# Denominators apart from numerators, feature weights reordered by GpSimd, and a reshuffled plan in a gated mix of two attentions

## The chip, the core and the metric

The kernel runs on one core of one Trainium2 chip. The metric is the device time of one execution in microseconds (us). The core has five engines that run at the same time: TensorE (PE) multiplies matrices, its weight loads being shown apart as PEld; ScalarE (ACT) does exponentials; VectorE (DVE) and GpSimd (POOL) do elementwise work; SyncE (SP) issues most of the transfers (DMAs). Results of PE go to eight PSUM banks, everything else lies in SBUF.

## The reference

The inputs are 2048 tokens of 512 features, in 32 heads of 16.

```python
g = sigmoid((x * gate_w).sum(-1, keepdims=True))
# A: softmax attention
q, k, v = heads(x @ A_wqkv)
a = softmax(q @ k.T * Dh**-0.5) @ v          # per head, 2048 x 2048 scores
a = merge(a) @ A_wo
# B: linear attention with a learnt feature map
q, k, v = heads(x @ B_wqkv)
pq, pk = q @ w_phi, k @ w_phi                # per head, 16 x 16
phi_q = concat(softmax(pq), softmax(-pq)); phi_k = the same of pk
kv, z = phi_k.T @ v, phi_k.sum(tokens)       # per head, 32 x 16 and 32
b = merge(phi_q @ kv / (phi_q @ z + 1e-6)) @ B_wo
out = g * a + (1 - g) * b
```

## The kernel before

**Branch A.** A score unit is 128 keys by 512 queries of one head; four heads side by side make a pack (one 32-row strip of PE each), 16 packs make a group, and there are 32 groups, 512 packs, 2048 units. PE computes the scores of two units (`_qk`, matmul at line 993) into a ring of four PSUM banks, ACT takes the exponential of both at once into `ET` (`_exp`, line 1041), and PE multiplies the result with the values into the accumulator of the group (`_pv`, `_values`, line 1100). Some units take another way: PE computes their scores into one of the other four banks (`vqk`), DVE forms the exponential's bits (line 900) and corrects them (`v_step`, line 925), and PE multiplies the result (`vs`) with the values (`pvx`). How many of a group's 64 units go to DVE is the list `NUMS` (line 847). A finished group is transposed out of PSUM by DVE (line 1121), normalised, brought back by SP's transfers and multiplied with `WoA`.

**Branch B.** The weights of q and k are first multiplied with the feature weights `wphi` (`_b_fuse`, line 1216): eight groups of four matmuls, whose moving operand is `wphi`, 128 columns each. Head and feature order is changed by the way in which the matmul reads `wphi`. Then, for pairs of 128-token tiles, `_b_pair` computes the features: a projection, POOL's negation (line 1274), maxima and subtraction on DVE, an exponential on ACT (line 1283), sums on DVE and POOL, POOL's reciprocals and ratios (`_b_ratio`), and a product on DVE (line 1329). Eight pairs are keys (`_b_kv` accumulates them); eight pairs are queries, which SP transposes into `phiT` (`_b_phit`, line 1388). `_b_kvbd` masks the accumulated sums into `kvbd`: for each of eight groups of four heads, 68 columns, in which each head has 16 numerator columns and one denominator column behind them. `_b_num` makes, for each tile of queries and each half of the heads, four matmuls of 68 columns into one bank (line 1406); DVE then forms the denominators (line 1418), takes reciprocals (1426) and multiplies (1427) into `onB`, which SP transposes (line 1450) for the matmul with `WoB`.

**The order of the work** is not written by hand. Each operation is given an engine, a cost, dependencies, and a rank `prio`, mostly a due time counted in packs (`K0`, `Q0`, `NDUE`, `QDUE`, `KDUE`, `VDUE`). `Plan.order` simulates the five queues with these costs, takes at each step what can start first, and among what can start then the lowest rank; the outcome is five fixed queues, in which each instruction waits for semaphores. PE's fill (matmuls with a zero operand, line 1107, and pads, line 1013) is added where the streaming of the last `SPAN` us would fall under the shares `SHARE`, `FLOOR` or `PAD`. `_late` keeps other PE work from delaying the next scores. `c_pe(n)`, line 531, is the planner's cost of a matmul of n columns.

Of the kernel before, what the change touches and what calls it, by code (L numbers as in the profile page):

```python
# [7 lines left out]
ALU = mybir.AluOpType  # L8
AX = mybir.AxisListType

P = 128
# [54 lines left out]
class Plan:  # L66
# [6 lines left out]
    SWITCH, PASS, STEP = 0.105, 0.2155, 0.004  # L73
    SPAN, SHARE, FILL = 3.3, 0.55, 0.2155
    PAD, PADS, OVER = 0.45, 3, 0.1
    SLIP, GAPS, FLOOR = 0, 0.7, 0.44

# [32 lines left out]
    def op(self, eng, fn, cost, reads=(), writes=(), deps=(), name="", prio=0.0, rel=-99, kind="full",  # L110
# [27 lines left out]
        return o  # L138

    def _late(self, end):  # L140

        k = self.n_qk
        if k >= len(self.qks) > 0:
            x = self.exps[-1]
            if self.last.end is not None or x.end is None and self.exps[-2].end is None:
                return False
            done = self.exps[-2].end + x.cost if x.end is None else x.end
            return end > done + self.LAT["ACT"] + self.MORE["ACT", "PE"] - self.SWITCH + self.TAIL
        if k < 2 or any(d.end is None for d in self.qks[k].deps):
            return False  # L150
        x = self.exps[k - 1]
        if x.end is None:
            if self.exps[k - 2].end is None or any(d.end is None for d in x.deps):
                return False
            done = max([self.exps[k - 2].end] + [d.end + d.lat for d in x.deps]) + x.cost
        else:
            done = x.end
        return end > done - self.LAT["PE"] - self.PASS - self.SWITCH + self.SLIP

    TAIL = 9.0  # L160
    NEAR = 0.05
    SAME = 100
    OPEN = 2
    HURRY, FREE = 20, 20
    PORT = ("v_step", "b_neg", "b_max", "b_sub", "b_sum", "b_total", "b_mul", "n_mul", "n_den", "kvbd")
# [230 lines left out]
class _Kernel:  # L396
# [9 lines left out]
    URGENT, AHEAD, SOON, REST = 4, -(1 << 30), 4, 6  # L406
    QDUE, KDUE, VDUE = 24, 17, 11
    P_Q, P_MUL, P_NEG = 1, 1, 1
    P_REC, P_SUM = 0, 4
    P_BACK, RATIO, BV = 1, 1, 8  # L410
    P_M, P_BMUL, CHUNKS = 0, 0, 2
    GDUE = 26
# [4 lines left out]
    LAST, FIRST_OUT, NEXT_OUT, DEP_OUT = 0, 8, 0, 2  # L417
    ALONE, EARLY = 12, 6
    PVP = 10
# [13 lines left out]
    def build(self):  # L433
        with ExitStack() as ctx:
            self._memory(ctx)
            p = self.plan
            p.pad = lambda ot: lambda e: self._fill(e, ot)
            p.free_banks = [(b, 0.0, []) for b in range(self.NRING, 8)]
            self._loads()
            self._consts()  # L440
            self._projections()
            self._branch_b()
            self._attention()
            p.qks, p.exps = self.qks, self.exps
            p.order()
            p.finals = self.stores
            p.emit(self.nc, ctx)
# [132 lines left out]
    def _consts(self):  # L580
# [29 lines left out]
        self.b_wphi0 = B()  # L610
        z = op("POOL", lambda e: e.memset(self.wphi[:], 0.0), 0.6, prio=-30)
        parts = []
        phi = self.B_w_phi.rearrange("(c h) d f -> h d c f", h=8)
        for hh in range(8):
            parts.append(lambda e, hh=hh: e.dma_start(self.wphi[16 * hh:16 * hh + 16, :, 16 * hh:16 * hh + 16], phi[hh]))
        self._shared_dma("wphi", parts, self.b_wphi, -5, [z])
        self.dma("SP", "wob", lambda e: e.dma_start(self.WoB[:], self.B_wo.rearrange("(q p) n -> p q n", p=P)),
# [228 lines left out]

    NUMS = (6, 10, 12, 14, 14, 16, 13, 15, 14, 17, 16, 13, 17, 15, 19, 16, 11, 18, 14, 17, 19, 14, 17, 14, 15, 20, 14, 20, 12, 16, 20, 14)

    def _plan_vector(self):

        NT, away = self.NT, []
        for g in range(self.NPACK // NT):
            n = self.NUMS[g]
            away += [4 * (NT * g + 1 + (2 * k + 1) * (NT - self.REST) // (2 * n)) + (len(away) + k) % 4 for k in range(n)]
        batches = [away[k:k + self.PACK] for k in range(0, len(away), self.PACK)]
        self.hooks = {}
        for k, units in enumerate(batches):
            due = max(units[0] / 4 - self.LEAD, self.VMIN)
            self.hooks.setdefault(max(0, int(due) - 4), []).append(
                lambda k=k, units=units, due=due: self._vector_batch(k, units, due))  # L860
        for n in range(1, 4 * self.NQC):
            self.hooks.setdefault(max(0, 32 * n - 30), []).insert(0, lambda n=n: self._proj_q(*divmod(n, 4)))
        self.away = set(away)
# [291 lines left out]

    NDUE = 23
    K0, SK, Q0, SQ = 30.0, 11.5, 214.0, 15.25

    def _branch_b(self):
# [6 lines left out]
        self.b_kv = [B() for _ in range(2)]  # L1166
        self.b_kvbd, self.b_onB, self.b_rinvB = B(), [B(), B()], [B(), B()]
        self.b_numB, self.b_numR = [B(), B()], B()
# [24 lines left out]
        for ch in range(NQC):  # L1193
            for tt in (0, 2):
                t = 4 * ch + tt
                due = self.Q0 + self.SQ * t
                phi = self._b_pair(0, t, due)
                for k in range(2):
                    self._b_phit(tt + k, phi, k, due + 12 + 2 * k)
                    self._b_num(t + k, self._num_due(t + k))  # L1200
                    self._b_out(tt + k)
# [4 lines left out]
    def _b_fuse(self, s, due):  # L1206
# [4 lines left out]
        for c in range(4):  # L1211
            job = Job()

            def mm(e, c=c, job=job):
                for cp in range(4):
                    ins = e.matmul(self._bank(job)[:, P * cp:P * cp + P], self.WT[:, cp, P * c:P * c + P],  # L1216
                                   self.wphi[:, cp, :].rearrange("p (g i f) -> p g f i", g=2, i=4), start=True, stop=True)
                return ins
# [24 lines left out]
    def _b_pair(self, s, t0, due):  # L1243
# [25 lines left out]
        def chain(ops, off, bufs):  # L1269
            for name, cost, fn, *spare in ops:  # L1270
# [5 lines left out]
                self.P_NEG * 1.1),  # L1276
               ("b_max", two(1024), lambda e: e.tensor_tensor(tree, x[:, :, 0:8], x[:, :, 8:16], ALU.max))]  # L1277
              + [("b_max", two(128 * n), lambda e, n=n: e.tensor_tensor(tree[:, :, 0:n], tree[:, :, 0:n],
                                                                       tree[:, :, n:2 * n], ALU.max)) for n in (4, 2, 1)]
              + [("b_sub", two(2048), lambda e: e.tensor_tensor(x, x, spread(tree[:, :, 0]), ALU.subtract))],  # L1280
# [3 lines left out]
           name="b_exp", prio=due + 1)  # L1284
        chain([("b_sum", two(1024), lambda e: e.tensor_tensor(half, x[:, :, 0:8], x[:, :, 8:16], ALU.add))]  # L1285
              + [("b_sum", two(128 * n), lambda e, n=n: e.tensor_tensor(half[:, :, 0:n], half[:, :, 0:n],  # L1286
# [60 lines left out]
    def _b_kv(self, t, slot, due):  # L1347
        op = self.plan.op
        for hf in range(2):
            job = Job()  # L1350

            def mm(e, hf=hf, job=job):
                for g4 in range(4):
                    gg = 4 * hf + g4
                    for k in range(2):
                        ins = e.matmul(self._bank(job)[:, 68 * g4:68 * g4 + 68],
                                       self.bq[:, slot, k, P * gg:P * gg + P], self.VB[:, (t + k) % 4, gg, :],
                                       start=(k == 0), stop=(k == 1))
                return ins
            m = op("PE", mm, 8 * self.c_pe(69), reads=[self.b_bq[slot], self.b_VB[t % 4], self.b_VB[(t + 1) % 4]],  # L1360
                   name="kv", prio=due, acquire=job)
            acc = self.kvacc[:, hf, :]
            if t == 0:
                op("DVE", lambda e, acc=acc, job=job: e.tensor_copy(acc, self._bank(job)[:, 0:272]), self.c_dve(272),
# [6 lines left out]
    def _b_kvbd(self, due):  # L1371
        op = self.plan.op
        bm = self.bm
        for hf in range(2):
            acc = self.kvacc[:, hf, :].rearrange("p (g v) -> p g v", g=4)
            dst = self.kvbd[:, 4 * hf:4 * hf + 4, :].rearrange("p g (i v) -> p g i v", v=17)
            op("DVE", lambda e, acc=acc, dst=dst: e.tensor_tensor(
                dst[:, :, :, 0:16], acc[:, :, 0:64].rearrange("p g (i d) -> p g i d", i=4),
                bm[:, None, :, None].to_broadcast([P, 4, 4, 16]), ALU.mult), 0.45,
               reads=[self.b_kv[hf], self.b_bm], writes=[self.b_kvbd], name="kvbd", prio=due)  # L1380
            op("DVE", lambda e, acc=acc, dst=dst: e.tensor_tensor(
                dst[:, :, :, 16], acc[:, :, 64:68],
                bm[:, None, :].to_broadcast([P, 4, 4]), ALU.mult), 0.15,
               reads=[self.b_kv[hf], self.b_bm], writes=[self.b_kvbd], name="kvbd", prio=due)

    def _b_phit(self, tt, slot, k, due):
# [4 lines left out]
        self.n_phit += 1  # L1391

    def _b_num(self, t, due):

        op, tt, slot = self.plan.op, t % 4, t % 2
# [35 lines left out]
        if self.P_M:  # L1431
# [17 lines left out]
        b_onB.writers, b_onB.readers = muls, []  # L1449
        self.dma("SP", f"ontb{t}", lambda e: e.dma_start(  # L1450
            self.onTB[:, :, tt * TOK:tt * TOK + TOK], self.onB[:, slot, :], transpose=True), cost=1.25, reads=[b_onB],
            writes=[self.b_onTB[tt]], prio=due + 1, lat=1.6)

# [100 lines left out]
```

## Time and profile before

| | us |
|---|---|
| median of 3 runs (780.72 to 781.92) | 781.41 |
| the profiled execution, its own time | 781.93 |
| its span, first to last instruction | 780.1 |
| ACT busy | 753.0 |
| PE busy | 754.9 |
| DVE busy | 711.2 |
| POOL busy | 208.9 |

The profile is of one execution. Its page has the busy time of each engine, the span in 40 slices of 19.5 us (each digit the busy share in tenths, PEclk the granted clock of PE in tenths of full speed), the chain of work that ended last, and groups of instructions: line, engine, operation, output and input tiles, shapes, count, then busy us, mean ns of one, and the idle time just before them with what ended it. A matmul's mean is its latency; a run of matmuls is pipelined, so the distance from one start to the next is shorter. Further views are stretches of the span with the busy time of each engine, a timeline of merged instructions, and the waits of one engine for another.

### The profile page before, as it was taken

What the parts mean: (1) busy time and instruction counts of PE and PEld (TensorE: products, weight loads), DVE (VectorE), ACT (ScalarE), POOL (GpSimd) and SP (SyncE); (2) the same over time, 40 slices, a digit from 0 to 9 for tenths busy, and PEclk for the clock granted to TensorE, in tenths of its full rate; (3) what the DMA queues carried; (4) which work ended last, traced back from release to release, by engine and by line L of the source; (5) the groups of instructions that cost most, each with busy time, mean ns of one, the idle gap of its engine ahead of it and who ended that gap; (6) DMA issues with size and microseconds to landing.
All of it is one profiled execution on the core that took longest, in us unless ns stands there. A gap on an engine that the chain in (4) does not pass through costs nothing.

```text
span 780.1 us, 16892 instructions
## 1 busy us (share of the span) xinstructions
PE 754.9 (97%) x7047; PEld 218.5 (28%) x7111; DVE 711.2 (91%) x1158; ACT 753.0 (97%) x807; POOL 208.9 (27%) x300
## 2 busy tenths in 40 slices
PE   8999999999999999999999999999999999999998
PEld 3322223322222222222222222222222222222222
DVE  3864898899999999999998999999999999999994
ACT  6996899999999999999999999999999999999996
POOL 2210034601533234414234132130424231140000
PEclk9995999999999999999999999999999999999999
DMA  9501010000000000010111103112020312102010
GB/s 221 131 2 28 1 14 5 12 1 8 9 1 9 8 4 12 2 14 2 15 36 43 27 21 35 35 32 26 15 42 14 40 30 49 21 8 35 15 16 28
DMA packets 89180, 20.78 MB, mean 27 GB/s; under 512 B 83472, under 2 KB 88592, under 8 KB 89104
## 3 DMA queue, kind: packets, MB, share of 16 engines
q1 hardware_dynamic: 87232, 18.92, 13.5%
q8 instruction: 56, 0.92, 0.5%
q10 hardware_dynamic: 1872, 0.79, 0.4%
q14 instruction: 20, 0.16, 0.1%
HBM read 4.21 MB, written 2.10 MB: 8 GB/s over the span
## 4 chain that ended last, share of the span: by engine, by line
ACT 74%; PE 19%; DVE 5%; DMA 1%; issue 1%
ACT ET L1041 71%; PE ps L993 6%; PE ps L1100 5%; PE ps L677 4%; ACT bq L1283 3%; PE ps L788 2%; DVE vs L900 2%; DVE vs L925 1%; PE ps L1216 1%; DMA xT<-in_A_x_dram 1%; DVE bq L1256 0%; DVE btree L1277 0%; DVE ghB L841 0%; PE ps L685 0%; PE ps L724 0%
## 5 line engine op out<-in xcount | busy, mean ns | idle before, releaser
L1041 ACT ACTIVATE ET<-ps 128x1024 bf16<-128x1024 f32 (+1 forms) x785 | 725.3, 1165 | 13.4 <-PE ps L993 13.0
L900 DVE TENSOR_SCALAR vs<-ps 128x512 uint16<-128x512 f32 x482 | 312.5, 682 | 25.0 <-PE ps L993 23.5
L993 PE MATMUL ps<-qT,kT 32*128 32x512 bf16 (+1 forms) x2052 | 317.2, 387 | 10.9 <-ACT ET L1041 5.9
L925 DVE TENSOR_SCALAR vs<-vs 128x2048 uint16<-128x2048 uint16 (+2 forms) x242 | 233.8, 976 | 1.2
L1100 PE MATMUL ps<-vs,V 128*32 128x512 bf16 x1928 | 211.3, 385 | 0.6 <-DVE vs L925 0.3
L1100 PE MATMUL ps<-ET,V 128*32 128x512 bf16 x1566 | 196.6, 390 | 0.3 <-DVE vs L900 0.2
L993 PEld LDWEIGHTS ps<-qT,kT 32*128 32x128 bf16 x2052 | 77.7, 91 | 317.7 <-ACT ET L1041 291.5
L1286 POOL TENSOR_TENSOR btree<-btree 128x512 f16<-128x512 f16 (+1 forms) x32 | 37.7, 1180 | 187.5 <-DVE btree L1285 186.5
L1100 PEld LDWEIGHTS ps<-ET,V 128*32 128x32 bf16 x1566 | 49.1, 94 | 82.4 <-issue 73.5
L1107 PE MATMUL ps<-kT,zero 128*32 128x512 bf16 x664 | 66.5, 384 | 0.0
L1100 PEld LDWEIGHTS ps<-vs,V 128*32 128x32 bf16 x1928 | 48.2, 95 | 51.2 <-issue 31.1
L1274 POOL TENSOR_SCALAR bq<-bq 128x1024 bf16<-128x1024 bf16 x16 | 20.3, 1266 | 138.3 <-DVE bq L1256 94.5
L677 PE MATMUL ps<-WB,xT 128*128 128x512 bf16 x169 | 51.9, 383 | 2.7 <-issue 2.2
L1138 POOL TENSOR_TENSOR T<-T,rinv 128x512 bf16<-128x512 f32 x15 | 17.3, 1156 | 109.4 <-DVE rinv L1136 109.4
L767 POOL TENSOR_SCALAR qT<-qtmp,mask 128x512 bf16<-128x512 bf16 x30 | 25.8, 866 | 45.3 <-DVE qtmp L762 44.9
L677 PE MATMUL ps<-xT,WA 128*128 128x512 bf16 x95 | 32.9, 401 | 2.5 <-issue 1.6
L1121 DVE STREAM_TRANSPOSE T<-ps 128x512 f32<-128x512 f32 x32 | 22.7, 710 | 13.1 <-PE ps L1100 13.0
L1283 ACT ACTIVATE bq<-bq 128x2048 bf16<-128x2048 bf16 x16 | 32.9, 2056 | 0.0
L1256 DVE CAST bq<-ps 128x512 bf16<-128x512 f32 x32 | 21.7, 681 | 1.7 <-PE ps L677 1.7
L1107 PEld LDWEIGHTS ps<-kT,zero 128*32 128x32 bf16 x664 | 15.9, 94 | 19.3 <-issue 17.5
L805 POOL TENSOR_SCALAR V<-V 128x544 bf16<-128x544 bf16 x16 | 12.7, 793 | 30.3 <-DVE V L798 30.1
L1280 DVE TENSOR_TENSOR bq<-bq,btree 128x2048 bf16<-128x2048 bf16 x16 | 19.5, 1220 | 0.1
(86 smaller groups left out, 414.1 us busy)
## 6 DMA issues: line engine op xcount, KB each, us to landing
T<-T SPq DMA_DIRECT2D x240, 8.0 KB, 1.8
WB<-in_B_wqkv_dram SPq DMA_DIRECT2D x1, 1536.0 KB, 7.1
out_dram<-WB SPq DMA_DIRECT2D x12, 128.0 KB, 1.7
WA<-in_A_wqkv_dram SPq DMA_DIRECT2D x2, 384.0 KB, 5.0
WoB<-in_B_wo_dram SPq DMA_DIRECT2D x1, 512.0 KB, 3.8
WoA<-in_A_wo_dram SPq DMA_DIRECT2D x1, 512.0 KB, 4.8
WA<-in_A_wqkv_dram ACTq DMA_DIRECT2D x2, 128.0 KB, 3.5
WA<-in_A_wqkv_dram ACTq DMA_DIRECT2D x1, 256.0 KB, 5.0
```

The lines of the kernel that those rows point to most:

```text
L677: return e.matmul(out, lhs, rhs, start=start, stop=stop)
L767: x = self.plan.op("POOL", lambda e, side=side: e.tensor_scalar(self.qT[:, s0 + side, :], tmp, self.mask[:, side:side + 1], 0.0, op0=ALU.m ...
L900: bits = lambda e, to, src: e.tensor_scalar(to, src, SCALE * LOG2E * 128.0, float(ORIGIN), op0=ALU.mult, op1=ALU.add)
L925: o = op("DVE", lambda e, k=k, src=src, dst=dst: e.tensor_scalar(dst, src, float(STEPS[k - 1]), None, op0=ALU.add), 0.16 + k * n * QCH * 0 ...
L993: return e.matmul(out[:, cols], self.kT[32 * i:32 * i + 32, cp, kt * TOK:(kt + 1) * TOK], self.qT[32 * i:32 * i + 32, s, cols], start=True ...
L1041: o = plan.op("ACT", lambda e: e.activation(self.ET[:, a % NS:a % NS + n, cols], self.ps[:, a % NR:a % NR + n, cols], ACT.Exp, scale=SCALE ...
L1100: ins = e.matmul(self._bank(ot)[32 * i:32 * i + 32, :], v[:, v0:v0 + 32], tile, start=(kt == 0), stop=(kt == self.NT - 1), tile_position=( ...
L1107: ins = e.matmul(self._bank(ot)[32 * i:32 * i + 32, :], self.zero[:], self.kT[:, 0, 0:QCH], start=False, stop=False, tile_position=(0, 32 ...
L1121: t1 = op("DVE", lambda e: e.transpose(T1[:, side].rearrange("p b s -> p (b s)"), src()), 0.735, deps=last, writes=[b_T1[side]], name="n_t ...
L1256: [lambda e, b, k=k: e.tensor_copy(bq[:, k].rearrange("p (g s v) -> p g s v", g=8, s=2)[:, :, 0, :], b.rearrange("p (g v) -> p g v", g=8))],
L1283: op("ACT", lambda e: e.activation(flat, flat, ACT.Exp), 1.789, reads=[b], writes=[b], name="b_exp", prio=due + 1)
L1286: + [("b_sum", two(128 * n), lambda e, n=n: e.tensor_tensor(half[:, :, 0:n], half[:, :, 0:n], half[:, :, n:2 * n], ALU.add), (n <= self.P_ ...
```

## The change

It has these parts:

- `wphi` is loaded into `onB[:, 0]`, which is not in use then, and POOL copies it into `wphi` in the order in which the matmul wants it; line 1216's matmul then reads its 128 columns one after the other.
- `kvbd` keeps the same 68 columns, but with 64 numerator columns first and four denominator columns behind. A new `_b_den` makes the denominators of two tiles in one bank by 16 matmuls of four columns, DVE turns them into reciprocals (two operations of 32 elements, one reciprocal of 64), and `_b_num` makes eight matmuls of 64 columns into one bank and one product of 512 columns.
- `NUMS` sums to 488 instead of 482.
- `Plan.shift` adds to each rank a small amount, of up to three packs, drawn from the operation's name and a table of seeds by stage.
- Due times, fill shares and a few other settings of the planner get new values. Options that the new code also has and that keep the former work (`KV2`, `P_MAX`) are 0.

```diff
-    SPAN, SHARE, FILL = 3.3, 0.55, 0.2155
-    PAD, PADS, OVER = 0.45, 3, 0.1
-    SLIP, GAPS, FLOOR = 0, 0.7, 0.44
+    SPAN, SHARE, FILL = 3.0, 0.58, 0.2155
+    PAD, PADS, OVER = 0.45, 2, 0.2
+    SLIP, GAPS, FLOOR = 0, 0.65, 0.46
...
+    def shift(self):
+        count = {}
+        for o in self.ops:
+            k = count[o.name] = count.get(o.name, 0) + 1
+            s = self.SEEDS[min(max(int(o.prio // 16), 0), 33)] if o.prio >= 0 else 0
+            if s:
+                h = sum(map(ord, o.name)) * 7919 + k * 104729 + s * 65537
+                h = (h ^ h >> 13) * 2654435761 & 0xFFFFFFFF
+                o.prio += (s % 3 + 1) * (((h ^ h >> 16) & 1023) / 511.5 - 1)
...
-    TAIL = 9.0
+    TAIL = 0.0
...
-    HURRY, FREE = 20, 20
+    HURRY, FREE = 20, 30
...
-    QDUE, KDUE, VDUE = 24, 17, 11
+    QDUE, KDUE, VDUE = 20, 17, 14
...
+    DEN, KV2, P_MAX = 1, 0, 0
+    REND = 5
...
-    ALONE, EARLY = 12, 6
+    ALONE, EARLY = 12, 10
...
-        z = op("POOL", lambda e: e.memset(self.wphi[:], 0.0), 0.6, prio=-30)
+        raw = self.onB[:, 0, :]
+        z = op("POOL", lambda e: e.memset(raw, 0.0), 0.6, prio=-30)
...
-            parts.append(lambda e, hh=hh: e.dma_start(self.wphi[16 * hh:16 * hh + 16, :, 16 * hh:16 * hh + 16], phi[hh]))
-        self._shared_dma("wphi", parts, self.b_wphi, -5, [z])
+            parts.append(lambda e, hh=hh: e.dma_start(
+                raw.rearrange("p (c j) -> p c j", c=4)[16 * hh:16 * hh + 16, :, 16 * hh:16 * hh + 16], phi[hh]))
+        self._shared_dma("wphi", parts, self.b_wphi0, -5, [z])
+        op("POOL", lambda e: e.tensor_scalar(
+            self.wphi[:].rearrange("p c (g f i) -> p (c g) f i", f=DH, i=4),
+            raw.rearrange("p (g i f) -> p g f i", i=4, f=DH), 1.0, 0.0, op0=ALU.mult, op1=ALU.add), 0.8,
+           reads=[self.b_wphi0], writes=[self.b_wphi], name="wphi_p", prio=5)
...
-    NUMS = (6, 10, 12, 14, 14, 16, 13, 15, 14, 17, 16, 13, 17, 15, 19, 16, 11, 18, 14, 17, 19, 14, 17, 14, 15, 20, 14, 20, 12, 16, 20, 14)
+    NUMS = (6, 10, 12, 14, 14, 15, 13, 16, 13, 20, 17, 13, 16, 13, 19, 21, 10, 18, 12, 16, 19, 13, 17, 16, 15, 20, 12, 19, 17, 16, 23, 13)
...
-    NDUE = 23
+    NDUE = 11
...
+                for k in range(2):
+                    if self.DEN and not k:
+                        self._b_den(t, self._num_due(t) - 1)
                     self._b_num(t + k, self._num_due(t + k))
...
-                                   self.wphi[:, cp, :].rearrange("p (g i f) -> p g f i", g=2, i=4), start=True, stop=True)
+                                   self.wphi[:, cp, :], start=True, stop=True)
...
+    def _b_den(self, t, due):
...
+            for k in range(2):
+                for gg in range(8):
+                    ins = e.matmul(self._bank(job)[:, 32 * k + 4 * gg:32 * k + 4 * gg + 4],
+                                   self.phiT[:, gg, (tt + k) * TOK:(tt + k + 1) * TOK], self.kvbd[:, gg, 64:68],
+                                   start=True, stop=True)
+            return ins
+        self.o_den = m = op("PE", mm, 0.56, array=0.1, reads=[self.b_kvbd] + bufs, name="den", prio=due, acquire=job)
...
+                fn = lambda e, k=k, x=x, g=g: e.scalar_tensor_tensor(
+                    out=rinv[:, k], in0=x(), scalar=g, in1=self.eps[:, tt + k], op0=ALU.mult, op1=ALU.add)
...
+        d = op("DVE", lambda e: e.reciprocal(both, both), 0.3, deps=d, name="m_rec", prio=due - 20)
...
+            for gg in range(8):
+                ins = e.matmul(self._bank(job)[:, 64 * gg:64 * gg + 64], self.phiT[:, gg, tt * TOK:tt * TOK + TOK],
+                               self.kvbd[:, gg, 0:64], start=True, stop=True)
+            return ins
+        m = op("PE", mm, 8 * self.c_pe(64), array=0.2, reads=[self.b_kvbd, self.b_phiT[tt]], deps=[self.o_den], name="num", prio=due,
+               acquire=job)
+        op("DVE", lambda e: e.tensor_tensor(
+            self.onB[:, slot, :].rearrange("p (h d) -> p h d", d=DH),
+            self._bank(job).rearrange("p (h d) -> p h d", d=DH), rinv[:, :, None].to_broadcast([P, H, 16]), ALU.mult),
+            self.c_dve(512), reads=[self.b_rinvB[slot]], writes=[self.b_onB[slot]], deps=[m], name="m_mul", prio=due - 20,
+            release=job)
```

## The prediction

> **What bounds the kernel now.** I read four views in this order: the page's slices and its chain, the table of stretches, the timeline where ScalarE (ACT) has holes, and the DVE groups of the work that is rewritten.
>
> The page, of the kernel before:
> ```profile
> span 780.1 us, 16892 instructions
> PE 754.9 (97%) x7047; PEld 218.5 (28%) x7111; DVE 711.2 (91%) x1158; ACT 753.0 (97%) x807; POOL 208.9 (27%) x300
> ...
> ACT  6996899999999999999999999999999999999996
> ...
> PEclk9995999999999999999999999999999999999999
> ...
> ACT 74%; PE 19%; DVE 5%; DMA 1%; issue 1%
> ```
> ACT is the bound: the chain is 74% ACT. PE's 97% is no bound, since 664 of its matmuls (66.5 us busy, line 1107) are fill and it waits for ACT before the scores (291.5 us in the waits). The fourth slice is the odd one: the granted clock falls to 0.5 and ACT to 6.
>
> The table of stretches (busy us and instruction counts of PE, weight loads, DVE, ACT, POOL; then granted clock):
> ```profile
> 0.00:56.00 56.00, 52.77 (x395) 18.18 (x402) 35.59 (x56) 48.24 (x55) 12.16 (x25) 0.97 0.54 123
> 56.00:62.00 6.00, 5.84 (x36) 2.28 (x35) 5.30 (x9) 4.12 (x5) 0.00 (x0) 1.00 0.00 0
> 62.00:79.00 17.00, 16.67 (x70) 2.96 (x69) 6.24 (x9) 11.20 (x11) 0.00 (x0) 0.50 0.15 32
> 79.00:84.20 5.20, 5.04 (x35) 1.87 (x38) 3.52 (x6) 3.18 (x5) 0.00 (x0) 1.00 0.00 0
> 84.20:110.00 25.80, 24.07 (x204) 6.65 (x200) 23.60 (x41) 23.89 (x27) 3.86 (x4) 1.00 0.05 5
> 110.00:350.00 240.00, 234.53 (x2250) 69.06 (x2274) 227.13 (x353) 239.83 (x256) 85.42 (x121) 1.00 0.05 8
> 350.00:683.00 333.00, 325.09 (x3137) 92.21 (x3157) 324.48 (x553) 332.93 (x356) 96.31 (x133) 1.00 0.17 28
> 683.00:760.00 77.00, 74.58 (x819) 20.12 (x819) 76.17 (x123) 77.00 (x84) 11.17 (x17) 1.00 0.11 19
> 760.00:780.10 20.10, 16.32 (x120) 5.19 (x120) 9.15 (x16) 12.62 (x15) 0.00 (x0) 0.97 0.08 27
> ```
> Length less ACT busy gives ACT's idle time, row by row: 7.76 (loads), 1.88, 5.80, 2.02, 1.91, then 0.24 in the 650 us from 110 to 760, and 7.48 at the end: 27.1 of the span. Only what shortens ACT's work or closes the holes between 56 and 110 can pay.
>
> The timeline at the first hole:
> ```profile
> 56.85 1.04 PE L1216 MATMUL ps<-wphi,WT 128*128 128x128 bf16 x4
> ...
> 58.57 1.94 ACT L1041 ACTIVATE ET<-ps 128x1024 bf16<-128x1024 f32 x2 [0.39 <-PE ps L993]
> ...
> 59.12 2.80 PE L1216 MATMUL ps<-wphi,WT 128*128 128x128 bf16 x12
> ...
> 62.40 2.11 ACT L1041 ACTIVATE ET<-ps 128x1024 bf16<-128x1024 f32 x2 [1.89 <-PE ps L993]
> ```
> Twelve matmuls with the feature weights run without a break, ACT waits 1.89 us, and the clock halves from 62 to 79. The pitch is (2.80 - 0.40) / 11 = 0.218 us for 128 columns. Their moving operand is the one read with a stride; the planner charges 0.056 each (line 531), so it takes three groups for 0.67 us.
>
> **Part 1: the feature weights reordered by GpSimd.** Contiguous price: eight matmuls of 68 columns span 0.43 us, one lasting 0.20 (timeline at 403.55), so (0.43 - 0.20) / 7 = 0.033; two of 512 columns span 0.60, one lasting 0.39, so 0.21. On that line 128 columns take 0.057. 32 matmuls save 32 x (0.218 - 0.057) = 5.2 us of PE, and a group of four takes 0.23 us, which fits the 0.60 that the scores (0.32 of a 0.92 us exponential) leave. So the waits of 56 to 62 and 79 to 84.2 should go: 1.88 + 2.02 = 3.90.
> The halved clock follows the stretch 56.8 to 62 in which 16 of these matmuls occupy 1.04 + 2.80 = 3.84 us for 16 x 0.057 = 0.9 us of streaming, though PE counts as busy; no other stretch after the loads halves it. I take thin streaming as its cause, so 62 to 79 also fills: 5.80. Together **-9.7**, bounds 0 to -9.7.
> The added POOL pass is like line 805's (0.79 us) or 767's (0.87). POOL is busy 1.37 us between 40 and 60; the weights are issued by 27.5 us and land in 1.7, the first use is at 56.8: hidden, 0. Without that cover it costs 0.9 once. The staging in onB delays nothing, its first other use being at 405 us. SP's eight DMAs are the same.
> Next late, 84.2 to 110: 1.28 of its 1.91 us come behind DVE's transpose of line 1121, when DVE is clearing what piled up (DVE 23.60 of 25.80). DVE was idle 10.8 us under the halved clock; without it the pile is smaller. I take half, **-0.9**, bounds 0 and -1.9.
>
> **Part 2: 488 score tiles on DVE in place of 482.** Six units fewer on ACT are three exponentials at 723.2 / 781 = 0.926: **-2.8**, certain. On DVE six more cost 6 x (312.5 + 233.8) / 482 = +6.8 us.
>
> **Part 3: numerators and denominators apart.** DVE before (groups of the whole run):
> ```profile
> L1427 DVE TENSOR_TENSOR onB<-ps,rinvB 128x256 bf16<-128x256 f32 x32 | 12.7, 415 | 0.2
> L1426 DVE RECIPROCAL rinvB<-rinvB 128x16 f32<-128x16 f32 x32 | 7.0, 238 | 0.1
> L1418 DVE SCALAR_TENSOR_TENSOR rinvB<-ps,ghB,eps 128x16 f32<-128x16 f32 x32 | 6.5, 220 | 0.4 <-PE ps L1406 0.3
> ```
> 26.2 us. After: 16 multiplies of 512 at 0.68 (line 1233, 682 ns) are 10.9; 16 m_den of 32 elements at 0.23 (0.22 for 16 elements; line 1129 has 0.207 for 32) are 3.7; eight reciprocals of 64 elements at 0.56 (238 ns for 16, line 1136's 346 for 32, continued) are 4.5. 19.1 in all, -7.1, so DVE's sum with part 2 is about even. DVE holds nothing from 110 to 683, so the saving itself gives 0.
> On PE, sixteen 4-column matmuls per pair of tiles come on top, each at most the 0.033 of 68 columns and at least nothing: 0 to 0.53 per pair, 4.2 us in all; I take 0.53. It displaces fill, and one piece fits the 0.60. Numerators of 64 columns cost as before. PSUM banks are taken three times a pair instead of four. Value 0; if the piece is cut badly, line 1216's 1.04 us piece cost ACT 0.39, eight times 3.1.
> The numerators come due 12 packs earlier, and the denominator waits for both transposes phiT. Behind it in PE's queue stand the next scores. In five of eight pairs now, the first numerator already starts 2.7 to 3.7 us after the second phiT is issued, whose landing takes 3.2, and PE's waits for it total 0.8 us. I take **+0.4**; bounds 0 and 8 x 0.5 = +4 (0.5 the longest such wait).
>
> **Part 4: shifted ranks, due times, fill thresholds, the unit list.** No row prices a shuffle. ACT's 0.24 us from 110 to 760 caps its gain; a loss as dense as the 1.91 in 84.2 to 110 marks the other side. The nearest rows are the full ones: 0. Up to the 28th of 32 groups the new list has one unit fewer than the old, and the last four 69 instead of 62: 7.9 us more on DVE while ACT's time there shrinks 3.2. Against these 11.1 us stand 7.1 saved just before and 6.65 idle before the last transpose (timeline at 772.29): covered, 0; without the 7.1 it is 11.1 - 6.65 = +4.4. In the tail, the last exponential ends at 771.5 and 8.6 us follow; the two output matmuls before the last values (771.30, 0.6 us) may move either way: -0.3 to +0.5, taken 0.
>
> **Sum** on the profiled execution's 781.93 (span 780.1 and 1.83 around): -9.7 - 0.9 - 2.8 + 0.4 = -13.0, **768.9**. That execution lies 0.5 above the median 781.41; I leave this in the range.
>
> **The rivals.**
> A, the clock halves all the same: 62 to 110 stay, the direct waits go: 781.93 - 3.90 - 2.78 = 775.2. For it: PE is busy 5.84 of 6.00 us before the fall, so idleness isn't its cause and something else than the stride may be. Against it: nothing else there is unlike the other stretches. The Trainium skill ("TensorE: Matmul & The Clock Gate", section "HAM oscillation — how this bites in real kernels") has the abstract rule that PE keeps its clock if it has no idle gaps over about 3.4 us; by it the slow matmuls would not be guilty and A would follow. The trace disagrees with the rule so far: there is no such gap before 62.
> B, one such fall elsewhere, likeliest at a denominator, which keeps PE for half a microsecond with almost nothing streaming: 768.9 + 5.8 = 774.7. For it: thin streaming is my cause. Against: the clock stays 1.00 from 110 to 760 through 16 numerators.
> C, DVE becomes the bound in the last four groups: 768.9 + 4.4 = 773.3. For: DVE is busy 76.17 of 77 us there. Against: the work removed just ahead.
> D, slower: the denominators drop the clock repeatedly. At 5.8 a fall, 13.0 / 5.8 = 2.2, so three of eight make it slower (786.3), all eight 815. The same row speaks against it.
>
> **How the numbers follow.** The forecast 0.70 (own range 766 to 772.5: down by 1.0 of part 1, 0.24 of part 4, 0.3 of the tail, 0.5 to the median and 0.6 for the spread of the runs, 780.72 to 781.92; up by phiT's +4 in place of 0.4), A 0.07, B 0.11, C 0.06, D 0.06. The range 766 to 775 takes in forecast, B and C and leaves out A and D, 0.13. A measurement can tell about 0.2% from no change, 1.6 us. Faster 0.93 (all but D and a little), same 0.01, slower 0.06.
>
> **What would show it.** Four matmuls on wphi spanning near 0.6 us with their drain, PEclk without a 5 in the fourth slice, ACT full from 56 to 100; 778 exponentials of two units; onB in 16 multiplies near 0.68; no wait of the denominator's matmuls beyond 1 us. It is wrong if the clock has a 5 after the loads, or ACT idles over 3 us from 110 to 760.

## The result and the profile after

The changed kernel takes 769.13 us (median of 6 runs, 767.55 to 770.57) against 781.56 (780.07 to 784.62) for the kernel before beside it: a ratio of 0.9836 [0.9814, 0.9859], 12.4 us. The forecast was 768.9. Its profiled execution took 767.62 with a span of 765.6, 14.5 less than the 780.1 of before. The sum came out right; two of its terms did not.

The page of the changed kernel:
```profile
span 765.6 us, 17042 instructions
...
PE 739.6 (97%) x7149; PEld 219.6 (29%) x7220; DVE 711.6 (93%) x1110; ACT 749.1 (98%) x804; POOL 207.5 (27%) x301
...
ACT  6999999999999999999999999999999999999996
...
PEclk9999999999999999999999999999999999999999
```
The 5 in the fourth slice of PEclk is gone, and ACT's 6 and 8 behind it. DVE's total stands where the forecast put it (711.6 against 711.2).

The stretches (busy us and counts of PE, weight loads, DVE, ACT, POOL, then granted clock, DMA share and GB/s), of the changed kernel:
```profile
0.00:56.00 56.00, 53.13 (x405) 18.45 (x410) 36.02 (x57) 48.64 (x56) 12.31 (x26) 0.97 0.54 123
56.00:62.00 6.00, 5.84 (x44) 1.99 (x45) 5.93 (x10) 6.00 (x7) 0.00 (x0) 1.00 0.27 58
62.00:79.00 17.00, 16.84 (x162) 4.97 (x161) 13.95 (x22) 17.00 (x20) 0.00 (x0) 1.00 0.05 12
79.00:84.20 5.20, 4.92 (x32) 1.44 (x35) 5.17 (x9) 5.20 (x7) 0.00 (x0) 1.00 0.00 0
84.20:110.00 25.80, 24.21 (x199) 7.18 (x194) 24.18 (x43) 24.41 (x28) 11.00 (x16) 1.00 0.08 11
110.00:350.00 240.00, 234.46 (x2246) 69.04 (x2268) 228.76 (x353) 240.00 (x256) 81.06 (x116) 1.00 0.05 7
350.00:670.00 320.00, 309.86 (x3134) 91.21 (x3166) 313.48 (x496) 319.05 (x341) 92.43 (x130) 1.00 0.17 29
670.00:745.00 75.00, 73.36 (x808) 20.02 (x807) 72.05 (x108) 75.00 (x83) 10.67 (x16) 1.00 0.11 19
745.00:765.60 20.60, 16.98 (x138) 5.32 (x141) 12.09 (x22) 13.80 (x16) 0.00 (x0) 0.98 0.08 26
```
Length less ACT busy is again ACT's idle time: 7.36 up to 56, nothing from 56 to 84.2 (before 1.88 + 5.80 + 2.02 = 9.70), 1.39 up to 110 (before 1.91), 0.95 from 350 to 670 (a new hole), 6.80 at the end (before 7.48).

The matmuls on `wphi` and `kvbd`, on PE's timeline of the changed kernel:
```profile
55.42 0.62 PE L1241 MATMUL ps<-wphi,WT 128*128 128x128 bf16 x8
...
56.67 0.40 PE L1241 MATMUL ps<-wphi,WT 128*128 128x128 bf16 x4
...
397.41 0.54 PE L1440 MATMUL ps<-kvbd,phiT 128*128 128x4 bf16 x16
```
Eight now take 0.62 us, where four took 1.04 in the kernel before. The sixteen 4-column matmuls of the first pair of tiles take 0.54.

DVE's groups of the rewritten normalisation:
```profile
L1475 DVE TENSOR_TENSOR onB<-ps,rinvB 128x512 bf16<-128x512 f32 x16 | 10.5, 677 | 0.0
...
L1458 DVE RECIPROCAL rinvB<-rinvB 128x64 f32<-128x64 f32 x8 | 4.3, 542 | 0.0
...
L1451 DVE SCALAR_TENSOR_TENSOR rinvB<-ps,ghB,eps 128x32 f32<-128x32 f32 x16 | 3.8, 240 | 0.0
```
18.6 us in all; the forecast had 10.9 + 4.5 + 3.7 = 19.1.

### The profile page after: what moved, and what is told of

Its sections match the earlier page's. It is cut to its first block, busy times and chain, and to the rows that moved or that the text cites. A ratio compares the mean times of both kernels' runs of the same rounds, so it can differ in the third digit from the quotient of the medians.

```text
span 765.6 us, 17042 instructions
## 1 busy us (share of the span) xinstructions
PE 739.6 (97%) x7149; PEld 219.6 (29%) x7220; DVE 711.6 (93%) x1110; ACT 749.1 (98%) x804; POOL 207.5 (27%) x301
## 3 DMA queue, kind: packets, MB, share of 16 engines
q1 hardware_dynamic: 87232, 18.92, 13.4%
## 4 chain that ended last, share of the span: by engine, by line
ACT 76%; PE 15%; DVE 9%; issue 1%
ACT ET L1063 73%; PE ps L1015 5%; PE ps L1122 5%; PE ps L698 3%; ACT bq L1310 3%; DVE vs L922 3%; DVE vs L947 2%; PE ps L1129 1%; PE ps L689 1%; DVE onB L1475 1%; DVE T L1143 0%; DVE bq L1307 0%; DVE btree L1304 0%; DVE ghB L862 0%; DVE qtmp L783 0%
## 5 line engine op out<-in xcount | busy, mean ns | idle before, releaser
L1015 PE MATMUL ps<-qT,kT 32*128 32x512 bf16 (+1 forms) x2052 | 312.4, 385 | 13.1 <-ACT ET L1063 8.0
L947 DVE TENSOR_SCALAR vs<-vs 128x2048 uint16<-128x2048 uint16 (+1 forms) x244 | 235.4, 977 | 1.9 <-PE ps L1122 0.5
L1122 PE MATMUL ps<-vs,V 128*32 128x512 bf16 x1952 | 216.4, 384 | 1.4 <-DVE vs L947 1.4
L1122 PE MATMUL ps<-ET,V 128*32 128x512 bf16 x1560 | 194.5, 387 | 0.1
L1314 POOL TENSOR_TENSOR btree<-btree 128x512 f16<-128x512 f16 (+1 forms) x32 | 33.4, 1044 | 188.8 <-DVE btree L1312 188.0
L1129 PE MATMUL ps<-kT,zero 128*32 128x512 bf16 x628 | 63.4, 385 | 0.0
L1122 PEld LDWEIGHTS ps<-vs,V 128*32 128x32 bf16 x1952 | 49.8, 95 | 45.9 <-issue 27.5
L698 PE MATMUL ps<-WB,xT 128*128 128x512 bf16 x160 | 49.6, 383 | 2.8 <-issue 2.1
L698 PEld LDWEIGHTS ps<-WB,xT 128*128 128x128 bf16 x192 | 13.3, 97 | 25.3 <-issue 20.5
```

The costliest lines, as they stand in the source:

```text
L698: return e.matmul(out, lhs, rhs, start=start, stop=stop)
L947: o = op("DVE", lambda e, k=k, src=src, dst=dst: e.tensor_scalar(dst, src, float(STEPS[k - 1]), None, op0=ALU.add), 0.16 + k * n * QCH * 0 ...
L1015: return e.matmul(out[:, cols], self.kT[32 * i:32 * i + 32, cp, kt * TOK:(kt + 1) * TOK], self.qT[32 * i:32 * i + 32, s, cols], start=True ...
L1122: ins = e.matmul(self._bank(ot)[32 * i:32 * i + 32, :], v[:, v0:v0 + 32], tile, start=(kt == 0), stop=(kt == self.NT - 1), tile_position=( ...
L1129: ins = e.matmul(self._bank(ot)[32 * i:32 * i + 32, :], self.zero[:], self.kT[:, 0, 0:QCH], start=False, stop=False, tile_position=(0, 32 ...
```

## The reorder alone

The first question is how much of the 12.4 us belongs to part 1. The kernel before, with only this (shown in part; no rank, setting or list is touched):

```diff
-        z = op("POOL", lambda e: e.memset(self.wphi[:], 0.0), 0.6, prio=-30)
+        raw = self.onB[:, 0, :]
+        z = op("POOL", lambda e: e.memset(raw, 0.0), 0.6, prio=-30)
...
+        op("POOL", lambda e: e.tensor_scalar(
+            self.wphi[:].rearrange("p c (g f i) -> p (c g) f i", f=DH, i=4),
+            raw.rearrange("p (g i f) -> p g f i", i=4, f=DH), 1.0, 0.0, op0=ALU.mult, op1=ALU.add), 0.8,
+           reads=[self.b_wphi0], writes=[self.b_wphi], name="wphi_p", prio=5)
...
-                                   self.wphi[:, cp, :].rearrange("p (g i f) -> p g f i", g=2, i=4), start=True, stop=True)
+                                   self.wphi[:, cp, :], start=True, stop=True)
```

> The kernel before with one part of the change: the feature weights pass through onB and a copy by POOL, and the matmul reads them without a stride. The planner puts these matmuls at the same places, twelve of them in a row. My theory (thin streaming by slow matmuls halves the clock): no half clock after the loads, time 781.6 - 9.7 - 0.9 = 771 us, so this part alone is over three quarters of the change. Rival A (the clock halves for another reason, only the direct waits go): about 777.7. Rival that the planner's shuffle did it: 781.

768.24 us (767.79 to 769.75), a ratio of 0.9818 [0.9768, 0.9867]: all of the gain. The matmuls, and the three stretches that had the holes, in the kernel before with the reorder:
```profile
56.94 0.84 PE L1222 MATMUL ps<-wphi,WT 128*128 128x128 bf16 x12
```
```profile
56.00:62.00 6.00, 5.81 (x45) 2.08 (x44) 5.96 (x9) 6.00 (x8) 0.00 (x0) 1.00 0.40 87
62.00:79.00 17.00, 16.69 (x157) 5.16 (x157) 13.89 (x21) 17.00 (x20) 0.00 (x0) 1.00 0.01 2
79.00:84.20 5.20, 5.04 (x34) 1.44 (x33) 4.39 (x11) 5.20 (x8) 0.00 (x0) 1.00 0.00 0
```
Twelve matmuls stand at the same place as before and take 0.84 us in place of 2.80: (0.84 - 0.22) / 11 = 0.056 us each, where the strided ones took 0.218. ACT is full from 56 to 84.2, with the clock at 1.00. The Trainium skill ("Advanced Engine Details and Errata", section "SBUF Cachelines") says that state-buffer reads that go to another 16-byte line at each access are penalised; the strided read goes 32 bytes on from one element to the next within each four, and the 3.9-fold pitch agrees.

To see whether the other parts add anything, both kernels ran once more side by side.

> The changed kernel once more, beside the next run on the same chip. By the sum of the prediction it should lie 2.4 us under the kernel that has the reordered weights alone: three exponentials less, 2.8, and 0.4 for waits. Rival: all the other parts together give nothing, and the two agree within 1 us.

> The kernel before with the reordered weights alone, once more, as the partner of the run above: 771 by the prediction's terms (781.6 - 9.7 - 0.9), 768 if the earlier run of it holds.

The changed kernel: 767.65 (767.4 to 769.29). The reorder alone: 767.98 (767.83 to 769.68). No difference can be seen between them. The stretches that differ, first of the changed kernel, then of the reorder alone:
```profile
84.20:110.00 25.80, 24.21 (x188) 6.88 (x188) 23.17 (x41) 23.23 (x26) 10.95 (x16) 0.93 0.08 11
...
350.00:600.00 250.00, 242.58 (x2440) 71.53 (x2465) 245.44 (x389) 249.15 (x266) 77.12 (x110) 1.00 0.16 29
```
```profile
84.20:110.00 25.80, 24.33 (x205) 7.43 (x206) 25.23 (x41) 24.51 (x26) 11.31 (x18) 1.00 0.08 11
...
350.00:600.00 250.00, 244.19 (x2369) 69.74 (x2384) 243.28 (x417) 249.93 (x268) 75.85 (x104) 1.00 0.17 29
```
ACT idles 2.57 and 0.85 us here in the changed kernel (in the first, the clock has also fallen, 0.93), 1.29 and 0.07 with the reorder alone. The three exponentials are saved as forecast: their group (the exponential of two units, all of the run) is 721.0 us with the reorder alone and 718.2 in the changed kernel, -2.8. But ACT's total falls only by 1.7 (750.7 to 749.0) and its idle time grows by 1.1 (15.4 to 16.5), so 0.6 of span is left.

The fall of the clock at 91.9 us is no fixed part of the changed kernel: its first profile has the same order of matmuls there and keeps its clock. Around the place, first in the profile with the fall, then in the one without:
```profile
88.50:91.90 3.40, 2.11 (x16) 0.60 (x15) 3.25 (x7) 2.87 (x4) 1.73 (x2) 1.00 0.05 5
91.90:95.30 3.40, 3.40 (x24) 0.50 (x22) 2.51 (x5) 1.44 (x2) 0.00 (x0) 0.50 0.14 17
```
```profile
88.90:92.30 3.40, 2.46 (x16) 0.51 (x15) 3.25 (x7) 3.40 (x5) 2.18 (x3) 1.00 0.00 0
92.30:95.70 3.40, 3.00 (x27) 0.84 (x27) 3.37 (x7) 2.01 (x3) 0.00 (x0) 1.00 0.13 13
```
In both, PE waits 1.28 to 1.29 us for DVE. In the traces' record of the clock, its changes lie a whole number of 3.41 us apart, and the stretches above are laid out in these steps. In the first profile the whole wait lies in one step, and the clock is halved in the next; in the second the border of two steps divides it, and nothing happens. So one execution of this kernel can have a fall that another has not. Over the six runs of each, the mean granted clock is 0.996 to 0.998 in the changed kernel and 0.998 to 1.000 with the reorder alone, which is some 3.8 us more at half clock in the mean; at the 0.36 us per us found below for the kernel before, I estimate that this takes back about 1.4 us.

## What halves the clock

The forecast took thin streaming of PE as the cause of the halved clock. The rival was that the clock falls in this place anyway, or for any crowding of PE. First the kernel before with its strided matmuls, but with two dense matmuls of 512 columns ahead of each group of four; their results are overwritten (shown in part):

```diff
+                for _ in range(2):
+                    e.matmul(self._bank(job), self.xT[:, 0, 0:P], self.xT[:, 0, 0:QCH], start=True, stop=True)
                 for cp in range(4):
```

> The kernel before, strided reads and planner's order kept; ahead of each group of four strided matmuls two dense ones of 512 columns are added (0.43 us), whose result is overwritten. PE gets more work there, 3.4 us in all. If it is thin streaming that halves the clock, the clock stays at 1.0, the direct waits grow by up to 3.4 and the half clock's 5.8 go: about 779 us, no slower than before though work was added. If the stride itself or something else there halves the clock, the half clock stays and the time is about 785.

777.4 us (776.26 to 777.88), a ratio of 0.9923 [0.9901, 0.9944]: with 3.4 us of PE work more, the kernel is 5.6 us faster, and in all nine runs the mean clock is 0.997 or more, against 0.976 to 0.989 in the twelve runs of the kernel before beside them. Its page and ACT's timeline where the clock fell before:
```profile
PEclk9999999999999999999999999999999999999999
```
```profile
58.58 1.94 ACT L1041 ACTIVATE ET<-ps 128x1024 bf16<-128x1024 f32 x2 [0.83 <-PE ps L993]
...
63.59 11.10 ACT L1041 ACTIVATE ET<-ps 128x1024 bf16<-128x1024 f32 x12 [3.08 <-PE ps L993]
```
The direct waits are longer (3.08 where 1.89 stood), since PE has more to do, but the clock stays and twelve exponentials run on without a wait. So neither the stride as such nor the crowding halves the clock.

The other way round: the changed kernel, whose reads are contiguous, gets one extra piece in the middle of the run, either 160 matmuls of four columns or, as a twin of equal length, 19 matmuls of 512 columns. Neither result is used:

```diff
+        def extra(e):
+            for _ in range(160):
+                ins = e.matmul(self._bank(job)[:, 0:4], self.WoA[:, 0, 0:P], self.WoA[:, 0, 0:4], start=True, stop=True)
+            return ins
+        op("PE", extra, 0.224, reads=[self.b_WoA], name="extra", prio=240, rel=240, acquire=job, release=job)
```
and, in the twin,
```diff
+            for _ in range(19):
+                ins = e.matmul(self._bank(job), self.WoA[:, 0, 0:P], self.WoA[:, 1, :], start=True, stop=True)
```

> The changed kernel plus, in the middle of the run, 160 matmuls of four columns without a stride in one piece, about 4.1 us in which PE is busy and streams almost nothing; the planner counts them as 0.22 us. Direct cost about 3.5 us. Theory: the clock halves behind them for several windows of 3.4 us, a further 5.8 or so: 769 + 9.3 = 778. The rule that only idle gaps of PE cost it its clock: clock stays, 772.5.

> The same place and length with 19 dense matmuls of 512 columns (4.0 us) in place of the 160 thin ones; the planner counts them alike. The direct cost alone: clock stays 1.0, 772.5 by theory and rule alike. The difference to the run with thin ones is the price of one fall of the clock.

With the thin piece 797.26 us (795.96 to 798.5; 1.0185 [1.0142, 1.0228]); with the dense one four runs from 794.83 to 811.67, with mean clocks from 0.988 down to 0.963: both far more than the piece. An added operation makes the planner write another order for all that follows, and in both profiles ACT idles 10 to 11 us between 600 and 700 and some 17 behind it, far from the piece (the changed kernel has 0.1 and 6.8 there). The totals therefore tell nothing; the place itself does. PE's timeline and the stretches there, with 160 thin matmuls:
```profile
372.01 4.15 PE L1219 MATMUL ps<-WoA 128*128 128x4 bf16 x160
```
```profile
372.60:376.20 3.60, 3.60 (x145) 3.56 (x141) 1.97 (x5) 0.44 (x1) 0.00 (x0) 1.00 0.31 44
376.20:383.00 6.80, 6.44 (x41) 1.50 (x43) 2.85 (x7) 4.36 (x5) 0.00 (x0) 0.50 0.01 1
```
and with 18 of the 19 dense ones, which stand in one row:
```profile
372.55 4.05 PE L1219 MATMUL ps<-WoA 128*128 128x512 bf16 x18 [0.16 <-issue]
```
```profile
372.60:376.20 3.60, 3.60 (x17) 1.61 (x17) 2.29 (x5) 0.76 (x1) 0.00 (x0) 1.00 0.23 41
376.20:383.00 6.80, 6.80 (x68) 1.91 (x66) 4.50 (x10) 6.04 (x7) 0.00 (x0) 1.00 0.01 2
```
PE is busy 3.60 of 3.60 us in both. Behind the thin piece the clock is 0.50 for 6.8 us, behind the dense one 1.00. ACT idles 5.84 us from 360 to 400 with the thin piece and 3.60 with the dense one, so the fall costs 2.2 us for 6.8 at half clock. The Trainium skill ("TensorE: Matmul & The Clock Gate", section "HAM oscillation — how this bites in real kernels") bids one avoid idle gaps of PE of over 3.4 us. That is not enough here: the clock fell with PE busy throughout, because little streamed through it. How little is too little was not measured.

The matmul's stride was put back into the changed kernel, with POOL now copying `wphi` in its plain order, so that only the read differs:

```diff
-            self.wphi[:].rearrange("p c (g f i) -> p (c g) f i", f=DH, i=4),
-            raw.rearrange("p (g i f) -> p g f i", i=4, f=DH), 1.0, 0.0, op0=ALU.mult, op1=ALU.add), 0.8,
+            self.wphi[:].rearrange("p c j -> p (c j)"), raw, 1.0, 0.0, op0=ALU.mult, op1=ALU.add), 0.8,
...
-                                   self.wphi[:, cp, :], start=True, stop=True)
+                                   self.wphi[:, cp, :].rearrange("p (g i f) -> p g f i", g=2, i=4), start=True, stop=True)
```

> The changed kernel with the feature weights copied by POOL in their former order and read with the stride again, the planner's order untouched. Here the matmuls stand in pieces of 8, 4, 4 and 4, 8, 4 instead of 4, 12 and 4, 8, 4. If thin streaming halves the clock, the first 16 of them in 3.5 of some 6 us do it again: 767.7 + 13 = 781, with a half clock near 60 us and waits of ACT there. If it took the other order to do it, the direct waits alone, 2 to 4 us: 771.

779.82 us (775.25 to 785.24), a ratio of 0.9974 [0.9939, 1.0009] to the kernel before: the gain is gone. PE's matmuls on `wphi` and the stretch 56 to 84.2:
```profile
54.28 1.92 PE L1240 MATMUL ps<-wphi,WT 128*128 128x128 bf16 x8
...
56.78 1.04 PE L1240 MATMUL ps<-wphi,WT 128*128 128x128 bf16 x4
```
```profile
56.00:84.20 28.20, 27.71 (x169) 6.98 (x170) 17.46 (x26) 20.53 (x21) 0.00 (x0) 0.76 0.09 19
```
The clock halves again (0.76 in the mean, 13.7 us of it at 0.50), and ACT idles 7.67 where the changed kernel has nothing. POOL's copy is still made here (0.62 us), so it is the matmul's read that counts.

## The other parts

Since the reorder alone gives everything, each of the other parts was taken out of the changed kernel by itself. With the old list of units (`NUMS` of 482):

> The changed kernel with the former list of 482 tiles on DVE, everything else kept. By the prediction's price of part 2, 2.8 us more than the changed kernel: 772. Rival, from the two runs with an extra piece of PE work, whose order came out so that ACT idled 20 us late in the run: any change of the list reorders the plan, which may cost up to 20 us: 772 to 790, and holes of ACT after 600 us where DVE is late.

with `DEN = 0`, the former denominators and numerators:

> The changed kernel with numerators and denominators together again as before (four matmuls of 68 columns per half tile), everything else kept, 488 tiles too. DVE then has 7.1 us more; its idle time between 350 and 745 is 9.5 us, so by the sum 0 to +3: 769 to 772. Rival (DVE becomes the bound of the last groups, rival C): +4.4, 773.5, with ACT waiting there. Reordering of the plan may add to either, up to 20 us.

without the call of `p.shift()`:

> The changed kernel without the small shifts of the ranks; all settings, the 488 tiles, the separate denominators and the reordered weights kept. The prediction priced the shifts at nothing: 768. Rival, after the runs with another list and with denominators put back: the order with these settings is only good with these shifts, and without them ACT idles 5 to 25 us after 350 us: 773 to 793, the clock staying at 1.0 between 56 and 84 in either case.

and with every setting as before and no shift, so that of the change only the reorder, `DEN` and the list of 488 remain (shown in part):
```diff
-    SPAN, SHARE, FILL = 3.0, 0.58, 0.2155
+    SPAN, SHARE, FILL = 3.3, 0.55, 0.2155
...
-    QDUE, KDUE, VDUE = 20, 17, 14
+    QDUE, KDUE, VDUE = 24, 17, 11
...
-            p.shift()
...
-    NDUE = 11
+    NDUE = 23
```

> The changed kernel with every setting of the planner as before and no shifts: reordered weights, separate denominators and the 488 list remain. By the prediction's terms: 767.9 of the reordered weights alone less 2.8 for three exponentials, 765. Rival: the order that the planner finds is no better tuned than in the other runs, 770 to 790, with holes of ACT late in the run where DVE's tiles come late.

| kernel | us, median (lowest to highest) | ratio to before |
|---|---|---|
| changed kernel | 767.65 (767.4 to 769.29) | 0.9811 [0.9782, 0.984] |
| with 482 units | 793.04 (790.11 to 794.69) | 1.0117 [1.0072, 1.0163] |
| `DEN = 0` | 775.19 (773.89 to 779.35) | 0.9902 [0.987, 0.9934] |
| no shift | 788.29 (785.03 to 792.5) | 1.0085 [1.0052, 1.0118] |
| old settings, no shift | 783.07 (780.68 to 787.28) | 1.0021 [0.9991, 1.0051] |

Each is 7.5 to 25 us slower than the whole, and all are slower than the kernel before with the reorder alone. ACT's timeline with 482 units, and without the shift:
```profile
700.96 9.27 ACT L1063 ACTIVATE ET<-ps 128x1024 bf16<-128x1024 f32 x10 [9.69 <-PE ps L1122]
```
```profile
406.47 1.94 ACT L1062 ACTIVATE ET<-ps 128x1024 bf16<-128x1024 f32 x2 [4.54 <-PE ps L1121]
...
786.69 1.08 ACT L1595 ACTIVATE xT<-ps 128x512 bf16<-128x512 f32 x2 [12.69 <-PE ps L697]
```
With 482 units one wait of ACT alone is 9.69 us: ACT waits for a matmul with the values, while DVE is busy 14.83 of the 15 us from 690 to 705. Without the shift, ACT waits 4.54 us at 406, in a half clock that lasts from 404.7 to 414.9, and 12.69 at the end. With `DEN = 0` the end shows most (PE's last matmuls with the values, and DVE behind them):
```profile
769.55 0.62 PE L1122 MATMUL ps<-vs,V 128*32 128x512 bf16 x8
770.22 0.72 DVE L1143 STREAM_TRANSPOSE T<-ps 128x512 f32<-128x512 f32 x1 [6.18 <-PE ps L1122]
```
DVE's tiles were ready at 764.0; the matmuls stood behind output matmuls in PE's queue, and the last wait of ACT is 9.68 us, against 3.83 in the changed kernel.

With the old settings there is a fall of the clock as well, with this lead (stretches):
```profile
390.20:393.60 3.40, 3.40 (x43) 0.92 (x35) 3.40 (x5) 3.40 (x5) 0.00 (x0) 1.00 0.36 63
393.60:397.00 3.40, 3.03 (x18) 0.84 (x17) 3.40 (x7) 3.21 (x4) 0.00 (x0) 1.00 0.71 138
397.00:407.20 10.20, 9.87 (x75) 2.91 (x74) 7.53 (x13) 7.02 (x6) 0.00 (x0) 0.50 0.07 15
```
PE is busy 3.03 of 3.40 us before it, but with 18 matmuls and not 43: it waits in small steps for DVE's score tiles. This is not the whole loss, nor its largest piece. ACT idles 5.5 us from 350 to 420 (the changed kernel 0.1), but 14.2 behind 760 us, most of it in the last wait:
```profile
777.26 1.09 ACT L1595 ACTIVATE xT<-ps 128x512 bf16<-128x512 f32 x2 [11.29 <-PE ps L697]
```
The same wait is 12.69 without the shift, 9.68 with `DEN = 0` and 3.83 in the changed kernel. So the settings and shifts go with an order that loses less in the middle and at the end; which of them does it, and how, was not tried.

The hole that is left near 92 comes behind DVE, which does four small copies of the gate there. As a multiplication by 1.0 they might have been shorter; this was tried on the kernel before with the reorder (shown in part):
```diff
-            done.append(op("DVE", lambda e, i=i, lo=lo, hi=hi: e.tensor_copy(
+            done.append(op("DVE", lambda e, i=i, lo=lo, hi=hi: e.tensor_scalar(
```

> The kernel before with the reordered weights, and the four copies of the gate (line 841 of before, 0.48 us each) made by a multiplication with one instead of a copy; the planner's order untouched. ACT's last hole before 110 us (1.29, near 91) stands behind DVE there. If the multiplication takes some 0.2 us, DVE is 1.1 us earlier and the hole shrinks to a few tenths: 767. If it takes as long as the copy, nothing changes: 768.

768.76 us (767.75 to 771.31), no gain, and the hole of 1.27 us is unchanged. DVE's group:
```profile
L847 DVE TENSOR_SCALAR ghB<-gh 32x16 f32<-32x16 f32 x4 | 1.9, 486 | 0.1
```
The mean is 486 ns as before, but it mixes unlike ones. On the timelines of DVE and of POOL:
```profile
84.21 0.15 DVE L847 TENSOR_SCALAR ghB<-gh 32x16 f32<-32x16 f32 x1
84.71 1.65 DVE L847 TENSOR_SCALAR ghB<-gh 32x16 f32<-32x16 f32 x2
87.71 0.17 DVE L847 TENSOR_SCALAR ghB<-gh 32x16 f32<-32x16 f32 x1
```
```profile
84.27 1.04 POOL L1280 TENSOR_SCALAR bq<-bq 128x1024 bf16<-128x1024 bf16 x1 [41.04 <-DVE bq L1262]
85.28 1.06 POOL L1144 TENSOR_TENSOR T<-T,rinv 128x512 bf16<-128x512 f32 x1
```
Two of the four take 0.15 and 0.17 us. The other two, 1.65 us together, run beside two instructions of POOL, and each ends some 0.02 us after one of these. In the run without the shift, where POOL is busy beside the first of the four only, the shortest, the median and the longest time (ns) are:
```profile
L861 DVE COPY ghB<-gh x4: 165/170/987, 88.3 to 89.8; 32x16 f32<-32x16 f32 x4
```
So neither the copy as such nor its stride is slow: 0.99 us for the first, 0.17 for the other three. The long ones go with POOL's work at the same time. This is read off the traces; no run moved POOL's work away.

## Why the prediction was right, and where it was not

**Part 1, -10.6 in the sum, measured -13.4 in span (780.1 to 766.7).** The mechanism held at each step: the pitch (0.057 forecast, 0.056 measured), the two direct waits, the clock, POOL's hidden copy (1.09 us for the 0.8 to 0.9 forecast). ACT's 9.70 us of idle time from 56 to 84.2 are all gone, and of the stretch to 110 0.62 in place of 0.9; a hole near 92 stays, 1.27 us with the reorder alone and 1.39 in the first profile of the changed kernel, so ACT is not full up to 100 us. What was under-sized is what lies beyond the holes. ACT's *busy* time fell too, from 753.0 to 750.9: an exponential that had to wait shows 1.02 us in these traces and one in a run 0.92 to 0.93, and some 17 fewer have to wait, about 1.7 of the 2.1 us. So a hole takes more than its idle time, and the forecast counted idle time only. Another 1.35 us less are in the loads up to 56, where one execution shows a half clock and another none: the profile of before and the first of the changed kernel have it, the three with the clock at 1.00 up to 56 us (both of the reorder alone and the second of the changed kernel) have not. That is chance and no effect of the change.

**Part 2, "-2.8, certain", failed.** The exponentials' group did fall by 2.8, but not the time: ACT idles more at 84.2 to 110 and from 350 to 600, and against the reorder alone the changed kernel gains 0.6 us in span and 0.3 in the median, which is within the spread of the runs. ACT's work is a lower bound of the time; PE and DVE have to deliver as much faster, and DVE has the six tiles more. Taking work from the bound is no certain term. Which of parts 2, 3 and 4 opened the new holes was not separated: the reorder alone lacks all three. One piece of it, the lower mean clock, is estimated above at 1.4 us.

**Part 3** had its sizes right (18.6 us of DVE for 19.1, 0.54 us of PE per pair for 0.53). The wait for phiT, +0.4, did not come: 0.

**Part 4 was priced at 0 by "the nearest rows are the full ones".** For the settings on record that held, but the step hides that they hold only together: with one of them put back, or the list or `DEN`, the order costs 7.5 to 25 us. A price of 0 with a remark on the other side was no fair picture; a re-planned order that misses should have been a rival of its own on the slower side, at some 15 us. No row of before could give its size.

So the sum is right by luck: part 1 was 2.8 too small, half of that by a clock that happened to fall in one profile's loads, and part 2 was 2 to 3 too large. The mechanism of part 1, the reordered read and the clock behind it, was foreseen and is shown.

**The rivals.** A (the clock halves all the same) is refuted by the reorder alone, whose mean clock is 0.997 or more in all of its 10 runs and 1.000 in seven. B (one fall elsewhere) is seen in small: 3.4 us at half clock in the changed kernel's second profile, at 92 us and behind DVE's jam, not at a denominator, and a mean clock under 1.000 in all of its runs. C (the last four groups) is what `DEN = 0` shows, and by a different way: not DVE, but values queued behind output matmuls. D was not seen: the clock of the changed kernel stays 1.00 through all eight denominators, from 397 us on; sixteen 4-column matmuls of 0.54 us did not halve it, 160 in a row did.

## How much is the clock

Each execution has a mean granted clock, and the kernel before ran in 50 executions beside the experiments. Its time follows that clock:

| mean clock | executions | us |
|---|---|---|
| 0.995 | 1 | 775.9 |
| 0.991 | 6 | 777.5 to 778.6 |
| 0.988 to 0.989 | 10 | 779.8 to 780.6 |
| 0.985 to 0.986 | 6 | 781.2 to 782.2 |
| 0.982 to 0.983 | 12 | 783.0 to 783.7 |
| 0.980 | 9 | 784.1 to 785.2 |
| 0.978 | 5 | 785.2 to 786.0 |
| 0.976 | 1 | 787.0 |

With the time at half clock as 2 x (1 - mean clock) x span, which runs from 7.7 to 37.7 us, a straight line has 0.36 us per us at half clock and meets full clock at 773.5; the correlation is 0.990. So the clock fell in every one of the 50, the time at half clock differs from one to the next, and almost all of the spread goes with it. That time includes falls in the loads and at the very end, as the profile of before has them (at 10.8 and 778.8 us). The forecast's 5.80 for 17 us is 0.34 per us, close to it. Of the 13.6 us between 781.6 and 768.0, I estimate about 8 for the clock and 5.5 for the direct waits and what lies behind them; the 773.5 behind this is extrapolated, since no run of this kernel had the full clock throughout.

## What to carry to other kernels

Look at the stretch with a lower granted clock first, and then at how much data streamed through TensorE in the few microseconds ahead of it, not at its busy share: a strided moving operand can keep it busy and starve it at once. A term that takes work from the bounding engine is a bound and not a gain, as long as the order that feeds it is re-planned. A planner's settings belong to the work that they were found for, and one part of such a change can't be valued by taking it out. A group's mean can mix unlike instructions: look at the single ones, and at what other engines do beside them, before a price is put on an operation.

## What was not expected

- The halved clock ends after whole windows: 17.1 us in the profile of before, 13.7, 10.2, 6.8 and 3.4 in other kernels, all multiples of 3.41 (but for a fall that the end of the run cuts off). The Trainium skill ("TensorE: Matmul & The Clock Gate", section "What's actually happening") gives a free-running window of 3.413 us, which agrees. Why a fall lasts for one window or for five stays open: the 50 executions of the kernel before had 2 to 11 of them in all.
- A matmul's moving operand with elements 32 bytes apart takes 0.218 us for 128 columns, 3.9 times the contiguous 0.056.
- Falls came without any long wait of PE: 1.29 us is the longest in the window ahead of the fall at 91.9 us, and 0.97 us in the one ahead of the fall at 404.7 without the shift (PE busy 1.64 of 3.40 us there).
- One added operation of 4 us cost 27 us or more through the order that the planner then wrote. Why those orders are bad, and why the list, the shift, the settings and `DEN` fit only each other, was not settled; no run separates the planner's cost model from chance there.
